# A long-convolution and SwiGLU kernel: orders and issue times from a table, first-norm statistics on DVE, weights in column pieces

## The chip, the cores and the metric

One core of one Trainium2 chip. Times are device microseconds (us) of one execution. "PE" is TensorE (matmul), "PEld" its weight loads, "DVE" VectorE, "ACT" ScalarE, "POOL" GpSimd, "SP" SyncE, which here only issues DMAs. A time is the median of several executions; a ratio is the mean time of one kernel's fast runs over the mean of the other's fast runs in the same rounds, so it is not quite the ratio of the medians quoted beside it. The calls in which kernels were run together were made on different chips, so kernels of different calls are compared by their ratios to the kernel before. One rule of reading: a PE that is "busy" in the profile is not a PE at its peak, so I also count *PE work*, the matmul columns of a stretch divided by 2,400 per us. The rate is the 2.4 GHz that the Trainium skill states ("TensorE: Matmul & The Clock Gate", Part 1). The trace agrees: in the stretches that PE fills, it does 9.7 to 10.05 us of such work per 10 us. The whole kernel has 251.5 us of it.

## The reference

```python
def _A_ref(q, k, v, shift_k, ssm_k, ssm_D):       # S = 2048, D = 640, bf16
    k_shift = sum over t of k_pad[:, t:t+S] * shift_k[:, 3 - t]      # 4 taps
    kv = k_shift * v
    y = irfft(rfft(pad(kv)) * rfft(pad(ssm_k)))[:S]                  # causal long convolution
    return q * (y + kv * ssm_D)

x  = A_q
h  = x + _A_ref(layernorm(x), A_k, A_v, A_shift_k, A_ssm_k, A_ssm_D)
n  = layernorm(h)
h2 = h + (silu(n @ w_gate) * (n @ w_up)) @ w_down                    # F = 1728
```

## The kernel before: what the change touches

The sequence is worked in four blocks j of 512 positions, each in two column halves c of 320. A block's convolution is a chain: load k and v, form `kv` on DVE, a first transform on PE, evict it, re-shuffle it between partitions by DMA (`sb<-sb`), a second transform, evict, swap the partition halves by DMA, complex products on DVE, two inverse transforms with another re-shuffle between. Then come the residual, the second norm, transposes, and the FFN, whose gate and up matmuls are 512 columns wide. A block's FFN can't begin before its convolution ends, and the FFN is 175 of the 251.5 us of PE work. In the first stage of the kernel there is no FFN work, and PE can only wait for the chain.

The program is a list of operations with priorities and dependences. A scheduler inside the kernel's builder simulates the engines and fixes each engine's order; the engines then run in that order and wait for each other by semaphores.

```python
def schedule(self, dma_model, bias):          # greedy list scheduling at build time
    ...
    for e in ("pe", "dve", "act", "sp", "pool"):
        if free[e] > t + 1e-9: continue
        best = None
        for o in ready:                        # the ready operation of least priority number
            ...
        o.eng, o.start = e, t
        ...

def ln_act(l, j, prio):                        # first norm: statistics on ACT, two passes
    for b in range(4):
        ... a.activation(out=junk, in_=x_b, func=ACTF.Copy, accum_out=sum_b)
    ...                                        # negative mean on DVE
    for b in range(4):
        ... a.activation(out=junk, in_=x_b, func=ACTF.Square, bias=negm_b, accum_out=ss_b)
    ln_rstd(l, j, prio, True, range(4))

def load_weights():                            # on the Pool queue, at most two on their way
    for i in range(5):                         # pieces of 128 rows: each gate group needs all five
        for (nm, t, wd) in (("wg", WG, B_w_gate), ("wu", WU, B_w_up)):
            piece([(V(t, i * FM, FM), dram(wd, i * 128 * F, [[F, 128], [1, FM]]))], 426, [(t, i)], ...)
    ...                                        # last 64 columns, then w_down

def group(t, bank, w, st, col, ...):           # one gate or up group: 5 matmuls of 512 columns
    wr = ... [(w, d) for d in range(5)]        # waits for all five row pieces
```

## Time and profile before

The kernel before takes 342.67 us (342.43 to 344.55, three runs).

| | before |
|---|---|
| PE busy | 286.1 us, 83% |
| DVE busy | 236.5 us, 69% |
| ACT busy | 202.3 us, 59% |
| first matmul of 512 columns (FFN) | 96.1 us |
| PE work done by 96 us | 28.2 of 251.5 us |

The page of the kernel before, part 2: 40 slices of 8.6 us. A digit is the busy share in tenths, in PEclk the granted clock in tenths.

```profile
PE   2161675867688999899799999999989999999992
DVE  0876453579883999889899899988888481222320
ACT  4175974886979877594278967766396521222100
PEclk9996656695589999999999999999999999999997
DMA  7949999898534556526546432634701101000011
```

Through the first eleven slices PE is partly idle, and from the fourth to the eleventh its clock is mostly granted only in part, while the DMA engines are nearly full up to the tenth. From the 14th slice on PE is nearly full.

The same in three stretches, from the table of windows (after the stretch: length, then busy us and number of instructions of PE, PEld, DVE, ACT, POOL, then granted clock, DMA share, GB/s):

```profile
0.00:96.00 96.00, 53.91 (x252) 24.93 (x253) 60.19 (x94) 65.07 (x108) 30.39 (x44) 0.74 0.82 255
96.00:118.00 22.00, 19.98 (x103) 9.41 (x102) 15.56 (x25) 19.11 (x33) 1.96 (x2) 0.98 0.44 135
118.00:284.00 166.00, 159.76 (x1012) 92.36 (x1011) 147.01 (x236) 109.58 (x170) 16.90 (x20) 1.00 0.43 127
```

PE is "busy" for 53.9 us of the first 96 and does 28.2 us of work in them. The low clock accounts for part of that: 53.9 us at a granted share of 0.74 are 40 us at full clock. The rest is the rule of reading above. What it waits for between 20 and 100 us, from the waits (total us, times, longest):

```profile
PE ps L537 <- DMA sb<-sb: 16.5, 9, 6.4
PE ps L537 <- ACT sb L522: 8.4, 17, 1.2
```

The shuffles are the longest wait. Pairing issues and landings in the trace, a shuffle issued between 20 and 60 us lands after a median 4.8 us, and after 2.4 us from 200 us on. The groups of the two norms' statistics (count, busy us, mean ns, idle before):

```profile
L788 ACT ACTIVATE sb<-sb,stt 128x640 bf16<-128x640 bf16 x16 | 13.1, 824 | 2.4 <-DVE stt L784 2.4
L781 ACT ACTIVATE sb<-sb 128x640 bf16<-128x640 bf16 x16 | 11.6, 727 | 2.1 <-DMA sb<-in_A_q_dram 2.0
L743 DVE BATCH_NORM_STATS2 stt<-sb 128x6 f32<-128x320 bf16 x32 | 14.0, 478 | 0.1
```

### The profile page before, as it was taken

What the parts mean: (1) busy time and instruction counts of PE and PEld (TensorE: products, weight loads), DVE (VectorE), ACT (ScalarE), POOL (GpSimd) and SP (SyncE); (2) the same over time, 40 slices, a digit from 0 to 9 for tenths busy, and PEclk for the clock granted to TensorE, in tenths of its full rate; (3) what the DMA queues carried; (4) which work ended last, traced back from release to release, by engine and by line L of the source; (5) the groups of instructions that cost most, each with busy time, mean ns of one, the idle gap of its engine ahead of it and who ended that gap; (6) DMA issues with size and microseconds to landing.
All of it is one profiled execution on the core that took longest, in us unless ns stands there. A gap on an engine that the chain in (4) does not pass through costs nothing. (4 is left out here: it accounts for less than half of the span.)

```text
span 343.3 us, 4790 instructions
## 1 busy us (share of the span) xinstructions
PE 286.1 (83%) x1668; PEld 156.3 (46%) x1668; DVE 236.5 (69%) x367; ACT 202.3 (59%) x317; POOL 49.2 (14%) x66
## 2 busy tenths in 40 slices
PE   2161675867688999899799999999989999999992
PEld 0140222332343565467554445576444477444571
DVE  0876453579883999889899899988888481222320
ACT  4175974886979877594278967766396521222100
POOL 4332513331211022021000100020001010000000
PEclk9996656695589999999999999999999999999997
DMA  7949999898534556526546432634701101000011
GB/s 194 397 138 327 298 254 305 257 287 246 143 124 142 126 183 213 150 77 193 162 156 191 123 125 74 197 134 136 184 28 38 38 21 38 21 0 0 3 38 39
DMA packets 27196, 49.78 MB, mean 145 GB/s; under 512 B 3858, under 2 KB 19123, under 8 KB 27045
## 3 DMA queue, kind: packets, MB, share of 16 engines
q1 hardware_dynamic: 22130, 32.29, 30.1%
q0 software_dynamic: 4064, 16.37, 16.4%
q10 hardware_dynamic: 978, 0.82, 1.0%
q8 instruction: 13, 0.21, 0.3%
q14 instruction: 11, 0.09, 0.1%
HBM read 20.63 MB, written 2.62 MB: 68 GB/s over the span
## 5 line engine op out<-in xcount | busy, mean ns | idle before, releaser
L537 PE MATMUL ps<-sb 128*128 128x512 bf16 (+2 forms) x996 | 192.1, 344 | 4.0 <-DMA sb<-in_A_shift_k_dram 2.5
L546 DVE TENSOR_TENSOR sb<-sb 128x1280 bf16<-128x1280 bf16 (+1 forms) x208 | 158.8, 798 | 29.1 <-DMA sb<-in_A_k_dram 11.3
L522 ACT ACTIVATE sb<-ps 128x640 bf16<-128x640 f32 (+1 forms) x144 | 101.8, 750 | 54.3 <-PE ps L537 37.4
L537 PEld LDWEIGHTS ps<-sb 128*128 128x128 bf16 (+1 forms) x996 | 97.0, 98 | 79.5 <-DMA sb<-in_A_shift_k_dram 2.4
L537 PE MATMUL ps<-sb,tab 128*128 128x320 bf16 x496 | 101.2, 340 | 32.8 <-DMA sb<-sb 18.6
L546 DVE TENSOR_TENSOR sb<-ps,sb 128x640 bf16<-128x640 f32 (+2 forms) x64 | 60.3, 950 | 54.7 <-PE ps L537 48.2
L537 PEld LDWEIGHTS ps<-sb,tab 128*128 128x128 f16 x496 | 47.4, 106 | 82.4 <-DMA sb<-sb 23.6
L982 ACT ACTIVATE sb<-ps 128x1024 bf16<-128x1024 f32 (+2 forms) x32 | 29.2, 912 | 40.8 <-PE ps L537 40.8
L769 ACT ACTIVATE sb<-sb,stt 128x320 bf16<-128x320 bf16 (+1 forms) x43 | 29.3, 728 | 10.0 <-DVE stt L761 8.1
L759 POOL TENSOR_TENSOR stt<-stt 128x2 f32<-128x2 f32 (+1 forms) x12 | 13.0, 1082 | 106.1 <-DVE stt L758 106.0
L525 ACT ACTIVATE sb<-ps 128x640 bf16<-128x640 f32 x32 | 21.6, 700 | 4.5 <-PE ps L537 4.5
L640 PE MATMUL ps<-sb 128*128 128x128 bf16 x96 | 7.9, 242 | 11.6 <-DMA sb<-in_A_ssm_k_dram 11.6
L788 ACT ACTIVATE sb<-sb,stt 128x640 bf16<-128x640 bf16 x16 | 13.1, 824 | 2.4 <-DVE stt L784 2.4
L743 DVE BATCH_NORM_STATS2 stt<-sb 128x6 f32<-128x320 bf16 x32 | 14.0, 478 | 0.1
L640 PEld LDWEIGHTS ps<-sb 128*128 128x128 bf16 x96 | 6.9, 121 | 13.3 <-DMA sb<-in_A_ssm_k_dram 12.5
L781 ACT ACTIVATE sb<-sb 128x640 bf16<-128x640 bf16 x16 | 11.6, 727 | 2.1 <-DMA sb<-in_A_q_dram 2.0
L530 POOL DMA_DIRECT2D sb<-in_A_ssm_k_dram x12 | 7.8, 654 | 33.4 <-PE ps L640 26.6
L942 PE MATMUL ps<-sb 128*128 128x128 bf16 x80 | 6.9, 243 | 2.4 <-ACT sb L522 1.9
L530 POOL DMA_DIRECT2D sb<-in_A_k_dram x6 | 5.9, 982 | 18.9 <-DVE sb L546 18.9
L530 POOL DMA_DIRECT2D sb<-in_A_v_dram x6 | 4.7, 791 | 22.4 <-PE ps L537 22.4
L942 PEld LDWEIGHTS ps<-sb 128*128 128x128 bf16 x80 | 5.5, 109 | 5.0 <-ACT sb L522 3.9
L761 DVE TENSOR_TENSOR stt<-stt 128x2 f32<-128x2 f32 (+1 forms) x12 | 1.9, 156 | 5.9 <-POOL stt L759 5.8
(25 smaller groups left out, 38.9 us busy)
## 6 DMA issues: line engine op xcount, KB each, us to landing
sb<-sb SPq DMA_DIRECT2D x160, 160.0 KB, 3.1
sb<-in_A_k_dram POOLq DMA_DIRECT2D x6, 560.0 KB, 6.7
out_dram<-sb SPq DMA_DIRECT2D x16, 160.0 KB, 1.8
sb<-in_B_w_gate_dram POOLq DMA_DIRECT2D x5, 416.0 KB, 4.4
sb<-in_B_w_up_dram POOLq DMA_DIRECT2D x5, 416.0 KB, 5.6
sb<-in_A_v_dram POOLq DMA_DIRECT2D x6, 320.0 KB, 4.0
sb<-in_A_q_dram POOLq DMA_DIRECT2D x3, 640.0 KB, 7.2
sb<-in_A_ssm_k_dram POOLq DMA_DIRECT2D x6, 256.0 KB, 4.2
```

The source lines that it names most:

```text
L522: fns = {"act": lambda a: a.activation(out=dst(), in_=src(), func=ACTF.Copy), "dve": lambda v: v.tensor_copy(out=dst(), in_=src())}
L525: fns = {"act": lambda a: a.activation(out=dst(), in_=src(), func=ACTF.Copy, scale=scale), "dve": lambda v: v.tensor_scalar(out=dst(), in0 ...
L530: fns = [(lambda g, d=d, s=s: g.dma_start(d(), s())) for d, s in subs]
L537: return lambda t: t.matmul(o(), l(), r(), start=st, stop=sp)
L546: return lambda v: v.tensor_tensor(out=o(), in0=a(), in1=b_(), op=op)
L640: return t.transpose(B16(pt, b // 2, (b % 2) * CW + o_, 128), src, V(IDN, 0, 128))
L743: vec(dve1(CW, False), lambda v: v.bn_stats(st6(l, j, b, c), V(xt, b * D + c * CW, CW)), [(xt, (b, c))], [(ST, ("s", l, j % 2, b, c))], pr ...
L759: P.op({"pool": 0.4}, lambda g: g.tensor_tensor(out=y, in0=va, in1=stt[:, 288:288 + hi - lo], op=ALU.pow), c1 + [(ST, "half")], c3, prio, ...
L769: "act": lambda a: a.activation(out=dst(), in_=src(), func=ACTF.Identity, scale=rs(l, j, b), bias=tmv(l, j, 3)[:, b:b + 1])},
L788: P.op({"act": act_c(D) + 0.3}, lambda a, b=b, jt=jt: a.activation(out=V(jt, 0, D), in_=V(xt, b * D, D), func=ACTF.Square, bias=tmv(l, j, ...
L942: fns.append(lambda t, k=k, d=d: t.transpose(B16(pt, k, d * 128, 128), V(hn[k], d * 128, 128), V(IDN, 0, 128)))
L982: P.op({"act": act_c(n)}, lambda a: a.activation(out=dst(), in_=src(), func=ACTF.Silu), rd, wr, -1000, name=f"si{j}{i}")
```

## The change

Its intent: replace the greedy scheduler by orders found beforehand. Engine and planned start of each of the 1,227 operations come from a table in the source. The first norm's statistics move from ACT to DVE (`bn_stats`, as the second norm has them). The gate and up weights come in four column pieces each, so that a group waits only for its own columns, and most loads move from the Pool queue into SP's queue, among the shuffles. The old rule that at most two weight pieces are on their way goes too.

```diff
-    def schedule(self, dma_model, bias):
-        ...                                             # 90 lines of simulation
+    def replay(self, table):
+        raw = np.frombuffer(zlib.decompress(base64.b85decode(table)), np.uint8)
+        eng, start = raw[:n], raw[n:].view(np.uint16)
+        for o, e, s in zip(self.ops, eng, start):
+            o.eng, o.start = self.ENG[e], 0.01 * int(s)
+        ...                                             # orders and buffer slots by planned start
+        for o in self.ops:                              # pacing of transfers
+            if o.dma is None or o.start < 1.5: continue
+            held = [...]                                # planned ends of what it waits for anyway,
+            ...                                         # and of the entry before it in its queue
+            if held and max(held) > o.start - 1.0: continue
+            ...
+                o.deps.setdefault(self.ops[work[k][1]], 2)
-        def ln_act(l, j, prio):                         # Copy and Square with accumulation on ACT
+        def ln_x(j, prio):                              # bn_stats and aggregation on DVE
+            for b in range(4):
+                for c in range(2):
+                    ln_stats(0, j, b, c, xts[j], prio)
+            ln_dve(0, j, prio, range(4))
-            for i in range(5):                          # five row pieces each
+            for f0, f1 in ((0, 3), (3, 6), (6, 9), (9, 13)):      # four column pieces each
+                n = (f1 - f0) * 128
                 for (nm, t, wd) in (("wg", WG, B_w_gate), ("wu", WU, B_w_up)):
+                    piece([(V2(t, f0 * 128, FM, 5, n), dram(wd, f0 * 128, [[F, 128], [128 * F, 5], [1, n]]))], ...)
-                wr = ... else [(w, d) for d in range(5)]
+                wr = ... else [(w, col // 128)]
```

## The prediction

> **What bounds the kernel now (342.67 us).** Matmul columns counted by shape from the trace (540 of 512, 944 of 320, the rest 128), divided by the 2.4 GHz that the Trainium skill states ("TensorE: Matmul & The Clock Gate", Part 1), give an estimate of 251 us of TensorE work at full clock. The table of windows shows three stages:
>
> - 0 to 96 us, before the first FFN matmul: only 30 us of that work is done. From 20 to 96 us the granted clock is 0.67, PE 48 of 76 us busy, DVE 49, ACT 59, the DMA engines 82%. In the waits, PE stands longest for sb<-sb shuffles (16.5 us), which take a median 4.8 us to land from 20 to 60 us, 2.4 to 2.8 after 100: they share the DMA engines with 6.6 MB of weights. Critical is the chain of block 0 (shuffles, ACT evictions of 0.70 us, two norms).
> - 96 to 284 us: clock 1.00, DVE 163 of 188 us busy, TensorE doing 9 to 10 us of work per 10: PE and DVE limit together.
> - 284 us to the end: the last FFN, PE alone, then 6.5 us of final add, store and closing.
>
> **What the change does.**
>
> - First-norm statistics leave ACT: 16 Copy (0.73), 16 Square (0.82), 32 accumulator reads (0.19), about 31 us. DVE gains 32 bn_stats (0.48, 0.40 back to back) and 16 aggregations (0.17), about 15 us. The table gives DVE 423 operations; 367 plus these 48 is 415, so some 8 evictions or norms move there, about 5 us. DVE goes from 236.5 to about 257, ACT from 202 to about 165.
> - Weights come in column pieces, 768 to 1,024 bytes a run instead of 3,328; a gate group waits for its own columns only. Loads wait on planned compute, most on SP. The skill, "DMA: Bandwidth & Descriptors" (Issuing engines are not separate DMA queues), says that all share the same 16 engines, so I expect gain from timing, not bandwidth.
> - Ordering the PE operations by the table's planned starts, the first FFN group comes after 27 us of PE work instead of 30, block 0's transposes after 24 instead of 28; FFN groups alternate with convolution from there. Before the last block's transposes lie 207 us, after them 45 (now 53).
>
> **Where it lies on the path.** The gain is in the first stage: block 0 finishes at 68 to 75 us rather than 90, because ACT and the DMA engines are freed, and PE becomes full that much earlier. With the first FFN matmul at 72, 180 us of PE work at 95% lead to the last transposes at 262 to 268; 45 plus 7 give 314 to 320. DVE contradicts mildly: from 9.2 us, 242 us of work before the last transposes and 20 to 25 us of idle (now 52) give 272 to 276, thus 324 to 328. DVE takes over as the limit and eats part of the gain.
>
> **Prediction: 321 us, range 308 to 334. Faster by over 2%: 0.88; within: 0.09; slower: 0.03.**
>
> **What would show it.** First 512-column matmul near 72 us, clock 1.0 from there; no Square or accumulator reads on ACT; DVE about 257 us, over 80%; early shuffles landing in 3.5 us; weights landing until beyond 90 us; no PE wait for weights; a final FFN-only stretch of 45 us.
>
> **What would make it wrong.** DVE packed better than I allow (under 310); DMA landing later than planned, shuffles behind paced loads on SP's in-order queue (above 335); short descriptors making the weights late.

## The result

The changed kernel takes 327.69 us (324.61 to 328.75, four runs), ratio to the kernel before 0.9538 (0.9465 to 0.9611). It was run again, as `after_again` (325.26 us, ratio 0.9467) and `after_third` (327.66 us, 0.9542). Its own spread, 324 to 330 us, is wider than the effect of some experiments below.

| | before | after |
|---|---|---|
| PE busy | 286.1 us, 83% | 279.8 us, 86% |
| DVE busy | 236.5 us, 69% | 251.3 us, 77% |
| ACT busy | 202.3 us, 59% | 172.8 us, 53% |
| first FFN matmul | 96.1 us | 78.0 us |
| PE work done by 96 us | 28.2 us | 43.8 us |
| span of the profiled run | 343.3 us | 326.9 us |

The page after, part 2 (slices of 8.2 us):

```profile
PE   2366588549997499999999999998999999999992
DVE  1499989996981979999999989989998976024421
ACT  3068589874987158547477567774355302321100
PEclk9999769957999699999999999999999999999997
DMA  7957979896989346537562621555531200100001
```

PE reaches its first nine in the tenth slice (the 14th before), and DVE is nearly full from the third slice on. But in the 13th and 14th slices PE falls to 7 and 4, with a dip of the clock, and DVE to 1 in the 13th. The windows, same stretches as before:

```profile
0.00:96.00 96.00, 64.42 (x348) 32.50 (x349) 77.92 (x138) 65.42 (x97) 15.24 (x22) 0.88 0.84 258
96.00:118.00 22.00, 14.91 (x81) 7.88 (x80) 12.62 (x19) 10.77 (x17) 1.11 (x2) 0.84 0.62 157
118.00:284.00 166.00, 163.30 (x1033) 95.38 (x1031) 148.72 (x256) 92.05 (x128) 12.16 (x11) 1.00 0.41 126
```

By 96 us the changed kernel is 15.7 us of PE work ahead (43.8 less 28.2); its profiled span is 16.4 us shorter. So nearly the whole gain is made in the first stage, as predicted. It would be more, but for 96 to 118 us: PE is 14.9 us busy there, against 20.0 before. This profile is of the slowest of the four runs; the same stretch in the profile of `after_third`, the fastest of its six, is milder:

```profile
96.00:118.00 22.00, 17.58 (x99) 9.38 (x98) 16.04 (x24) 13.84 (x20) 2.25 (x4) 0.92 0.66 194
```

PE's waits between 20 and 100 us have shrunk:

```profile
PE ps L454 <- DMA sb<-sb: 6.8, 6, 1.9
PE ps L454 <- ACT sb L438: 6.8, 15, 0.9
```

Shuffles issued between 20 and 60 us now land after a median 2.6 us (4.8 before). The smaller pieces alone do not do it: with them under the greedy scheduler (`parts_greedy` below) the median is 6.0 us, and with row pieces under the table (`rows_table`) 3.5. The statistics are all on DVE, 64 instead of 32:

```profile
L660 DVE BATCH_NORM_STATS2 stt<-sb 128x6 f32<-128x320 bf16 x64 | 29.7, 482 | 0.1
```

**The stall.** The chain of waits, followed back from the last instruction, goes through it (start, us, what):

```profile
93.21 2.75 SPq L446
95.96 0.04 issue
96.00 9.53 DMA sb<-sb
105.53 0.02 issue
105.55 0.83 DVE sb L463
```

A swap is issued in two halves. SP needs 2.75 us to issue the first (its median is 0.58), so that the second is issued at 96.00 only, and this lands 9.5 us later. The timeline says what DVE and PE do meanwhile (start, us, engine, line, what, in brackets the idle time before and who ended it):

```profile
100.50 0.83 DVE L463 TENSOR_TENSOR sb<-sb 128x1280 bf16<-128x1280 bf16 x1 [2.95 <-DMA sb<-sb]
105.55 0.83 DVE L463 TENSOR_TENSOR sb<-sb 128x1280 bf16<-128x1280 bf16 x1 [4.22 <-DMA sb<-sb]
...
110.89 2.31 PE L454 MATMUL ps<-sb,tab 128*128 128x320 bf16 x8 [7.09 <-DVE sb L463]
```

And the loads issued around this swap:

```profile
89.82 0.59 SPq L446 DMA_DIRECT2D sb<-in_B_w_down_dram  x1
90.51 0.56 SPq L446 DMA_DIRECT2D sb<-sb  x1
91.17 0.54 SPq L446 DMA_DIRECT2D sb<-in_A_k_dram  x1
91.81 4.82 SPq L446 DMA_DIRECT2D sb<-sb  x4
93.29 1.29 POOL L446 DMA_DIRECT2D sb<-in_A_ssm_k_dram  x2 [8.28 <-PE ps L557]
94.58 0.87 POOL L446 DMA_DIRECT2D sb<-in_B_w_up_dram  x1
95.45 0.78 POOL L446 DMA_DIRECT2D sb<-in_B_w_down_dram  x1
96.23 0.89 POOL L446 DMA_DIRECT2D sb<-in_B_w_gate_dram  x1
96.67 0.59 SPq L446 DMA_DIRECT2D sb<-in_B_w_up_dram  x1
```

From the k load at 91.17 us on these are 2.1 MB of loads, with the swaps' own halves 2.8 MB, issued within 6 us, and a table of narrower windows has the DMA share at 1.01 from 92 to 107 us. From 107 to 118 it is 0.16.

**Plan against chip.** Each operation's planned start is in the table, so I could pair plan and trace operation by operation. This is the slip (measured start less planned start, us) of some PE operations in three runs; the last column, `best2`, is the best of the experiments.

```
operation                        planned   after   after_third    best2           
first filter transpose, block 0      5.3     5.8       5.6            5.9
a second transform, block 0, c=1    31.3     8.2       8.2            5.0
first transposes, block 0           60.5     9.9       9.5            6.6
first gate group, block 0           66.0    12.0      11.9           10.0
inverse of block 1, c=1             91.4    20.6      17.7           11.3
first transposes, block 1          128.9    23.0      19.7           14.0
first transposes, block 3          247.5    25.6      22.7           16.8
```

The plan is not a prediction of mine, it is part of the kernel; but the slip shows where the chip falls behind it. That is almost only before 118 us, while loads are on their way: 5.8 us by the first transpose, 6 more by the first gate group, 6 to 9 more from there to block 1's inverse, which is the stall. In the 120 us between the first transposes of block 1 and of block 3 only 3 are added.

**The pacing code does nothing.** The change's text says that loads are paced, and the code adds a wait on a compute operation to a transfer that has over 1 us of planned slack. I built the program and counted: of 192 transfers none gets such a wait, because for each the entry before it in its queue, or something it has to wait for anyway, is planned to end within 1 us of its start (three start too early to be asked). What paces the loads is their place in the queues among the shuffles.

### The profile page after: what moved, and what is told of

Its sections match the earlier page's. It is cut to its first block, busy times and chain, and to the rows that moved or that the text cites. A ratio compares the mean times of both kernels' runs of the same rounds, so it can differ in the third digit from the quotient of the medians.

```text
span 326.9 us, 4728 instructions
## 1 busy us (share of the span) xinstructions
PE 279.8 (86%) x1668; PEld 156.4 (48%) x1668; DVE 251.3 (77%) x423; ACT 172.8 (53%) x245; POOL 28.5 (9%) x34
## 3 DMA queue, kind: packets, MB, share of 16 engines
q1 hardware_dynamic: 37682, 45.17, 45.5%
## 4 chain that ended last, share of the span: by engine, by line
PE 55%; DVE 12%; DMA 11%; ACT 10%; issue 5%; SPq 4%; POOL 2%; ACTq 0%; DVEq 0%
PE ps L454 53%; DVE sb L463 10%; DMA sb<-sb 9%; ACT sb L438 8%; SPq L446 3%; DMA sb<-in_A_ssm_k_dram 3%; POOL stt L676 2%; DVE stt L660 1%; PE ps L848 1%; PE ps L557 1%; ACT sb L686 1%; ACT sb L892 1%; ACT sb L441 0%; ACT L892 0%; DVE stt L664 0%
## 5 line engine op out<-in xcount | busy, mean ns | idle before, releaser
L438 ACT ACTIVATE sb<-ps 128x640 bf16<-128x640 f32 (+1 forms) x140 | 97.7, 745 | 59.1 <-PE ps L454 55.4
L454 PE MATMUL ps<-sb,tab 128*128 128x320 bf16 x496 | 95.4, 326 | 28.0 <-DVE sb L463 10.1
L463 DVE TENSOR_TENSOR sb<-ps,sb 128x640 bf16<-128x640 f32 (+3 forms) x64 | 60.7, 952 | 36.8 <-PE ps L454 35.4
L686 ACT ACTIVATE sb<-sb,stt 128x320 bf16<-128x320 bf16 (+1 forms) x40 | 28.4, 734 | 16.8 <-DVE stt L678 15.0
L660 DVE BATCH_NORM_STATS2 stt<-sb 128x6 f32<-128x320 bf16 x64 | 29.7, 482 | 0.1
L676 POOL TENSOR_TENSOR stt<-stt 128x2 f32<-128x2 f32 (+1 forms) x12 | 14.6, 1223 | 149.7 <-DVE stt L675 106.9
L439 DVE COPY sb<-ps 128x1280 bf16<-128x1280 bf16 x6 | 4.9, 822 | 11.7 <-PE ps L557 7.9
L446 POOL DMA_DIRECT2D sb<-in_A_ssm_k_dram x6 | 4.1, 680 | 47.2 <-PE ps L557 30.0
L664 DVE BATCH_NORM_AGGREGATE stt<-stt 128x2 f32<-128x12 f32 x32 | 5.5, 192 | 0.0
L439 DVE CAST sb<-ps 128x640 bf16<-128x640 f32 x2 | 1.6, 824 | 3.5 <-PE ps L454 3.4
L564 POOL TENSOR_TENSOR sb<-sb 1x320 bf16<-1x320 bf16 x2 | 2.0, 1012 | 17.5 <-DVE sb L439 10.9
```

What stands on the lines that cost most here:

```text
L438: fns = {"act": lambda a: a.activation(out=dst(), in_=src(), func=ACTF.Copy), "dve": lambda v: v.tensor_copy(out=dst(), in_=src())}
L439: "dve": lambda v: v.tensor_copy(out=dst(), in_=src())}
L446: fns = [(lambda g, d=d, s=s: g.dma_start(d(), s())) for d, s in subs]
L454: return lambda t: t.matmul(o(), l(), r(), start=st, stop=sp)
L463: return lambda v: v.tensor_tensor(out=o(), in0=a(), in1=b_(), op=op)
L660: vec(dve1(CW, False), lambda v: v.bn_stats(st6(l, j, b, c), V(xt, b * D + c * CW, CW)), [(xt, (b, c))], [(ST, ("s", j % 2, b, c))], prio, ...
```

## The experiments

Two theories stood after the traces. Theory A: the gain comes from orders and issue times, and what is missing from it is lost where loads collide with shuffles and swaps on the DMA engines. Theory B, the prediction's own: DVE has become the limit, and DMA waits only show where it has slack. A third, for the gain, was the freed ACT.

Twelve runs follow. All were reported correct within the tolerance, also the one whose statistics are wrong. `MOVE` is a small dictionary of planned starts that overrides the table: `o.start = self.MOVE.get(o.name, 0.01 * int(s))`. All else stays as the table has it, so it changes an order, and for a load with over 1 us of slack it also makes the pacing wait come into being. In its names, `ident` is the identity matrix, `x` the input, `kin` a load of k, `kraw` of the raw filter, `wg`, `wu` and `wd` gate, up and down pieces, `gul0` and `gul1` the last 64 columns of up and gate, and `kte00` the first eviction of the filter's transposes.

### One part alone: first-norm statistics on DVE, greedy scheduler kept

```diff
 (kernel before)
-            ln_act(0, j, pb + (300 if j else 95))
+            ln_x(j, pb + (300 if j else 95))
```

> The kernel before with its own greedy list scheduling, and only the first norm's statistics taken to DVE (32 bn_stats and 16 aggregations in place of 16 Copy, 16 Square and their accumulator reads on ACT). Theory A (most of the gain is in the orders and in when loads are issued): between 1% faster and 1% slower, 339 to 346 us. Rival (freeing 31 us of ACT in the first stage is the gain): 8 us or more faster, under 335.

342.54 us, ratio 0.9958 (0.9877 to 1.0039; one slow run of four left out of the ratio). Its page shows the trade in the busy times:

```profile
PE 280.7 (83%) x1650; PEld 155.5 (46%) x1668; DVE 246.6 (73%) x415; ACT 179.5 (53%) x253; POOL 46.2 (14%) x66
```

23 us less on ACT and 10 more on DVE give nothing. Under the old scheduler the rival, that ACT was the gain, falls. The table with the statistics left on ACT was not tried.

### Two parts: column pieces as well, greedy scheduler kept

```diff
 (the version above)
-            for i in range(5):   ... five row pieces
+            for f0, f1 in ((0, 3), (3, 6), (6, 9), (9, 13)):   ... four column pieces
-                wr = ... [(w, d) for d in range(5)]
+                wr = ... [(w, col // 128)]
```

> The same plus the column pieces of the weights, still greedy. Theory A: all weights had landed at 75 us in the kernel before, well ahead of the first FFN matmul at 96, so pieces alone give nothing: within 2 us of the norm-only version. Rival (a gate group that waits only for its columns starts the FFN earlier): 4 us or more faster than the norm-only version.

341.54 us, ratio 0.9960 (0.9902 to 1.0019): within 1 us of the version above. Under the old scheduler the pieces are worth nothing, since all the weights had landed at 75 us, well before the first FFN matmul at 96. So the rest of the change makes the step from 0.996 to 0.954: the table with its orders, its issue times (with the end of the limit of two weight pieces) and SP's queue for the loads, alone or together with the two parts. These were not separated from each other.

### Column pieces undone under the table

```diff
 (kernel after)
-            for f0, f1 in ((0, 3), (3, 6), (6, 9), (9, 13)):   ... columns
+            for d0, d1 in ((0, 1), (1, 2), (2, 3), (3, 5)):    ... rows
-                wr = ... [(w, col // 128)]
+                wr = ... [(w, d) for d in range(5)]
+    MOVE = {'wg2': 47.0, 'wu2': 56.0}
```

> The changed kernel with row pieces of the weights again (runs of 3,328 bytes, every gate group waits for all eight); two pieces had to be planned earlier (at 47 and 56 us) since the order deadlocks otherwise. Theory A (the pieces matter only because they let the loads spread past the first FFN matmul): 0.85 MB more are loaded before the first FFN group, it starts 2 to 5 us later than in the changed kernel, total 1 to 6 us more. Rival (longer runs move faster and outweigh it): the same or less than the changed kernel.

329.50 us, ratio 0.9595, against 0.9538, 0.9467 and 0.9542 of the changed kernel: 0.5 to 1.3% slower, 2 to 4 us. It was run at another time. The intervals overlap, so the size is not certain; but the trace has the first gate group 5 us later (slip 17.1 us, against 12.0 and 11.9), as expected. Without the two moves the check for deadlocks refused the program: the table plans pieces of the weights after the first gate groups, and with row pieces these wait for them. The column pieces are thus what allows the table its late loads, and, as it seems, are worth a little only there.

### The start: the identity first

The first filter transpose is planned at 5.3 us and runs at 11.06. I took the identity matrix, which lands at 10.97 us behind the filter on ACT's queue, for the cause.

```diff
+    MOVE = {"ident": 0.6, "x0": 5.6, "kin10": 6.2}
```

> The identity matrix is issued first on ACT's queue, and the x and second k loads after the first v and filter loads. Theory A (the plan has the first transposes at 5.3 us, they start at 11.06 because identity and filter land at 10.97 and 9.92; all that follows inherits about 5 us): the first transposes at 8 to 10 us, everything 1 to 3 us earlier, total 1 to 3 us less than the changed kernel. Theory B (first-stage shifts are absorbed by slack before the FFN): within 1 us.

A miss. 325.06 us, ratio 0.9487, within the changed kernel's own spread (0.9467). The identity landed at 2.6 us, but the second part of the filter load now landed at 11.17 us instead of 9.92, and the transposes began at 11.2 us as ever. So which of the two was issued first does not matter. The DMA engines are full meanwhile (a share of 1.02 from 2 to 11 us, here and in the changed kernel), so the bytes that share them are the likely limit; no run took any away.

### The stall: six loads behind the swaps

```diff
+    MOVE = {"kin30": 81.0, "wu6": 83.0, "kraw21": 86.0, "wd6": 99.0, "gul1": 100.5, "gul0": 101.5}
```

> Six loads (k of block 3, raw filter of block 2, three weight pieces, one of them the small last up and gate columns) are planned after the two swaps at 92 to 97 us instead of around them. Theory A (the swap lands 12 us after its issue because 2.8 MB of loads share the DMA engines with it, and PE and DVE then stand for it): the swap lands within 5 us, the PE gap at 100 to 118 us shrinks by 7 to 10 us, total 317 to 321 us. Theory B (DVE's own work limits from here, the DMA wait only shows where slack is): total within 2 us of the changed kernel, 325 to 329, with DVE filling the gap.

323.46 us, ratio 0.9424, against 0.9467 of the changed kernel: 1.5 us less in the mean of the fast runs, which the intervals don't separate. The mechanism came out as theory A said: the swap was issued at 92.5 and landed at 97.1 us, and the slip of PE at block 1's inverse fell from 20.6 (17.7 in another run of the changed kernel) to 12.8 us. The size did not, because I had moved two small loads too far. A new wait shows in PE's waits:

```profile
PE ps L455 <- DMA sb<-in_B_w_up_dram: 3.2, 1, 3.2
```

That is the last gate group waiting for the last 64 columns of the weights. The down piece and these two had run into the next shuffles, and PE lost another 1.7 us right after.

### Only the two smallest of these loads later

```diff
+    MOVE = {"gul0": 101.5, "gul1": 100.5}
```

> Only the two smallest of those loads (82 KB each, runs of 128 bytes) are planned later. Theory A (bytes in the burst decide): little, 0 to 2 us off the changed kernel. Rival C (the many tiny runs of 128 bytes clog the queues): most of the gain of the six-load version, 5 us or more.

326.26 us, ratio 0.9525: no gain. The swap still needed 9.1 us to land, from 91.8 to 100.9. That the tiny runs of these two make the stall is ruled out as far as the swap's landing tells.

### DVE: more work, and less

```diff
 (kernel after, more)
+            if l == 0:                       # a second bn_stats into an unused place
+                fns.insert(0, lambda v: v.bn_stats(unused, V(xt, b * D + c * CW, CW)))
 (kernel after, less; wrong result on purpose)
-  v.bn_stats(st6(l, j, b, c), V(xt, b * D + c * CW, CW))
+  v.bn_stats(st6(l, j, b, c), V(xt, b * D + c * CW, CW if l else 16))
```

> The changed kernel with every one of the first norm's 32 bn_stats done twice (the extra result goes to an unused place): about 13 us more of DVE work. The prediction's theory (DVE takes over as the limit, only 20 to 25 us of it idle before the last transposes): total 10 to 13 us more. Theory A (after 118 us PE is the limit and the time lost is DMA waits): under 6 us more.

334.39 us, ratio 0.9748, which is 2.1 to 2.8 points above the changed kernel's ratios, 7 to 10 us. It was run at another time. DVE was busy 262.9 us, 11.6 more. So neither number was right: too much for theory A, too little for a pure DVE limit. (The edit also makes each of these operations wait for the last but one; DVE's idle time did not grow by it, as the numbers below show.)

> Wrong result on purpose: the first norm's 32 bn_stats read 16 elements instead of 320, which takes some 9 us of work from DVE. 11.6 us of added DVE work cost 7 to 10 us. If DVE is a full co-limit (theory B), as much is won back per us: 5 to 8 us less than the changed kernel. If DVE had only small slack and PE or DMA limits just below (theory A): 0 to 3 us less.

325.59 us, ratio 0.9484, against 0.9542 of the changed kernel: 2.0 us less in the mean, which the intervals don't separate, for 9.3 us less of DVE (242.1 busy). Here theory A's number held. Added DVE work costs 0.6 to 0.8 us per us, removed work returns 0.2. The traces tell where. From 9.2 us to block 0's first FFN transposes, DVE is busy 54.5 of 61.2 us in the changed kernel. With the added work it is busy 61.2 of 65.9, and these transposes come at 75.1 us instead of 70.4 (69.9 in `after_third`): most of the delay is made there. With work removed it is busy 50.0 of 61.1, and they come at 70.3, no earlier. So DVE has some 2 us of slack in the chain of block 0: more work uses it up and delays the chain, while less work only leaves DVE to wait for something else. In this run the swap of the stall was still issued at 92.8 and landed at 102.6 us.

### The changed kernel once more, for comparison

> The changed kernel unaltered, for comparison on the same chip. Both theories: 324 to 329 us, and again a stall of PE between about 96 and 118 us in which the last swap (sb<-sb) of block 1's second column half lands over 8 us after its issue.

325.26 us, ratio 0.9467. One of its four executions, the profiled one, took 1,574.82 us, left out of the ratio, though not of the median (the three fast runs have a mean of 324.86 us); see the last section. So this run's own profile can't tell of the stall.

> The changed kernel unaltered once more, as the base of this call: 324 to 329 us.

327.66 us, ratio 0.9542. In its profiled run, of 324.0 us, the swap landed 9.6 us after its issue (12.3 in the first profile of the changed kernel, of 326.9 us). The stall is there in each profile of a fast run, and its length varies: in `after_third` SP issued both halves in 0.59 us each, and PE's longest wait was 4.4 us, so some 2 of the 2.7 us between the two correspond to the slow issue of 2.75 us.

### Two sets of moves

```diff
+    MOVE = {"gul0": 13.0, "gul1": 13.3, "wg9": 45.6, "kin30": 81.0, "wu6": 83.0,
+            "kraw21": 86.0, "wd6": 104.0, "kte00": 9.2}
```

> Moves of planned starts only. The two small last-column loads go to 13 us, where the DMA engines were 61% busy; the last gate piece (655 KB) from 28 to 45.6 planned; the k load of block 3, the filter of block 2 and one up piece behind the swaps; one down piece far behind; and the first filter eviction on DVE behind the first two products, which were ready earlier. The six-load version removed the 96 to 118 us stall but made the last gate group wait 3.2 us for the small pieces and pushed bytes into the next swaps. Theory A (collisions of loads with swaps and shuffles): 4 to 8 us under the changed kernel of this call. Theory B (DVE's work limits): 0 to 2 us under it.

324.42 us, ratio 0.9459, against 0.9542: 2.9 us less in the mean of the fast runs (the intervals overlap), under what theory A had asked for. The swap landed after 3.9 us and the first stall was gone, but two others had opened. The gate piece moved to 45.6 delayed the shuffles at 55 us (the slip there rose from 6.5 to 10.0 us at once), and at 118 to 128 us two down pieces, block 3's k and two swaps met:

```profile
118.00:130.00 12.00, 8.13 (x37) 3.82 (x35) 7.74 (x11) 4.84 (x8) 0.00 (x0) 0.86 0.90 234
```

PE is busy 8.1 us of 12 there, with the DMA engines at 0.90. Loads moved out of one collision had run into the next.

```diff
+    MOVE = {"gul0": 13.0, "gul1": 13.3, "kin30": 81.0, "wu6": 83.0, "wg9": 85.0, "kraw21": 87.5,
+            "wd6": 97.8, "kin31": 112.0, "wd3": 92.0, "kte00": 9.2}
```

> The first set of moves took the stall at 96 to 118 us away, but a second one of some 5 us opened at 118 to 128 us, where two down pieces, block 3's k and two swaps met, and the 655 KB gate piece, moved to 45.6, cost as much near 55 us as it won near 35. This set puts that gate piece at 85, one down piece at 92, one at 97.8, and block 3's second k load at 112 planned. Theory A (collisions, each avoidable while the DMA engines have quiet stretches): both stalls gone, ratio to the kernel before 0.930 to 0.942, about 319 to 323 us. Rival (the DMA engines are so full before 118 us that every move opens another stall): 0.944 to 0.954, no better than the first set, with a new wait of PE or DVE of 4 us or more on a shuffle elsewhere.

318.41 us (316.68 to 319.94), ratio 0.9292 (0.9256 to 0.9328), the interval clear of all others. This version beats both kernels: 24 us less than the kernel before, and by the ratios 6 to 9 less than the changed one. It was run at another time. No operation was changed, only the places of nine loads and one eviction; six of the moved loads now have enough planned slack to get the pacing wait. Its windows:

```profile
0.00:96.00 96.00, 64.06 (x357) 33.38 (x358) 79.01 (x141) 67.10 (x99) 14.31 (x20) 0.88 0.85 261
96.00:118.00 22.00, 19.69 (x117) 10.47 (x116) 18.72 (x26) 15.45 (x24) 3.32 (x5) 1.00 0.93 264
118.00:284.00 166.00, 163.91 (x1024) 95.23 (x1023) 143.00 (x248) 87.85 (x121) 10.86 (x9) 1.00 0.37 110
```

From 96 to 118 us the DMA engines are *busier* than in the changed kernel (0.93 against 0.62, or 0.66 in `after_third`), and PE is busy 19.7 us instead of 14.9 (17.6), at full clock. The loads now fill the quiet time that the stall had left behind it. The swap was issued at 90.9 and landed at 94.6 us. The rival, that the DMA engines are too full for any move to help, falls. Not every term is separated: the eviction moved on DVE and the two small loads at 13 us came in both sets, and the slip at 36 us fell from 8.2 to 5.0 us there. What each of the ten moves is worth alone was not tried, nor the moves without the pacing waits that they brought into being.

## Why the prediction was right, and what in it was not

The time, 327.7 us, lay within the range of 308 to 334, and the gain was 15 us instead of 21.7.

- **"The gain is in the first stage" — right.** 15.7 us more PE work is done by 96 us, of a gain of 16.4 in the profiled runs.
- **"Because ACT and the DMA engines are freed" — half wrong.** Freeing ACT under the greedy scheduler gave 0.4%, within the noise. The DMA engines are not freed: 82% of the first 96 us before, 84% after. What changed under the table is that the early shuffles land in 2.6 instead of 4.8 us, and that more work is done early: DVE does 77.9 instead of 60.2 us in these 96 (9.5 of the 17.7 more are statistics and their aggregations).
- **"First 512-column matmul near 72 us" — 6 us too early.** It came at 78.0. The plan has the first gate group at 66.0 and the slip had grown to 12 us there: 5.8 at the first transposes, which wait for the first loads, the rest after them. That this rest is shuffles and swaps behind loads was not tested one by one.
- **The term that was left out: the stall at 96 to 118 us.** The prediction held "shuffles behind paced loads" only as a risk that would end above 335. It happened, at a smaller size: PE was busy 14.9 of 22 us. From the first FFN matmul to the last block's transposes PE needed 195 us for 177.5 us of work, 91% where I had put 180 us at 95%. Of the 17.5 us lost, 9.8 lie between 96 and 118 us (6.2 in `after_third`); from 118 to 284 us it did 159.2 us of work in 166, 96%.
- **"DVE takes over as the limit and eats part of the gain" — half right.** Added DVE work cost 0.6 to 0.8 us per us, so there is little slack. But it was not what held the changed kernel at 327: with the same DVE work the last set of moves runs at 318, and with 9.3 us less of it the kernel gained only 2.0. That the DVE path's 324 to 328 us hit the measured 327.7 is partly luck: it had 242 us of work from 9.2 us to the last block's transposes and 20 to 25 idle, and the trace has 235.5 and 28.4, so that two errors cancel (273.1 us, where it had 272 to 276). In the last set of moves 20.5 us of idle remain, and the transposes come at 264.3.
- **"Loads wait on planned compute" — wrong.** No transfer of the changed kernel gets such a wait; the order in the queue paces them.
- **"So I expect gain from timing, not bandwidth" — right.** The packets of the queues that carry the program's transfers took 47.5% of 16 engines' 343.3 us before and 50.2% of 326.9 after, 163 and 164 us: the shorter runs cost about nothing. "DMA: Bandwidth & Descriptors" (Issuing engines are not separate DMA queues) says that all queues end on the same 16 engines, and the stall fits it: the swap on SP's queue landed in 4.6 us instead of 12.3 once loads on both queues had been moved behind it (no run moved those of the Pool queue alone).
- Sizes that held: DVE 251.3 us busy (257 predicted; 77% where I said over 80), ACT 172.8 (165), the final stretch of FFN alone 45.5 us (45), no wait of PE for weights. The "30 us" of work that the prediction gives the first 96 us of the kernel before are 28.2 by the columns.

Open: how much of the table's gain is order, how much issue time and how much the change of queue; what holds the chain of block 0 when DVE has less to do; why one issue on SP took 2.75 us in one profile and 0.59 in another; and whether the statistics' move is worth more under the table than the nothing it was worth under the old scheduler.

## What to carry to other kernels

When a chain of DMA shuffles sets the pace, ask of every bulk load which shuffle it will meet: 2.1 MB of loads issued within 6 us around two swaps left PE idle for 7.1 us in one profile and 4.4 in another, and moving nine loads and one eviction was worth 6 to 9 us, while the statistics' move and the column pieces gave nothing clear of noise under the old scheduler. If a planned schedule exists, pair it with the trace operation by operation; the places where the slip grows are the list of things to mend, and a moved load must be followed to the next collision. And check in the built program that a mechanism which a change announces, here the pacing waits, is there at all.

## What the Trainium skill lacked or had wrong

- "DMA: Bandwidth & Descriptors" gives the time of a transfer by its size and names arbitration between queues, but no time for a small transfer that meets bulk loads. Here a 160 KB shuffle lands in 2.0 us at best, in a median 4.8 us beside the weights in the kernel before, and a swap 12.3 us after the start of its issue in the stall.
- The same page's back-pressure text is about remote DMA. Here the *issue* of a local DMA can be held up too: SP took 2.75 us for one issue in the stall (median 0.58). Why is open: the same issue took 0.59 us in `after_third`, and single issues of 1.2 to 1.6 us came at 155 to 160 us too, where the DMA engines were busy to about 0.3.
- The same page (Specifications) asks for runs of 512 bytes or more for line rate. Above it the trace of the changed kernel still shows a loss: a packet of 640 bytes took a median 32 ns, of 1,280 bytes 55, of 4,096 bytes 159, which is 20, 23 and 26 bytes per ns of one engine. The packets of 2,560 bytes don't fit this row: a median of 169 ns, 15 bytes per ns.
- No page has the duration of the norm statistics on DVE: 0.48 us for 128 x 320 bf16, 0.17 to 0.19 us for the aggregation. None has that of an accumulator read on ACT: 0.19 us each, beside an activation of 0.73 us.
- "TensorE: Matmul & The Clock Gate" warns (Part 1, "HAM trace caveats"; HAM is the monitor that gates the clock) that the clock records can be unreliable and the clock stuck at a quarter for over 50 us. One execution may be such a case, far longer, though no record of its clock shows it: it was of the changed kernel and took 1,574.82 us, with PE busy 99%, a mean matmul of 1,479 ns instead of 345 (128x512 and 128x320 together) and a weight load of 321 ns instead of 98, DVE's times unchanged, and a recorded granted clock of 1.0. It came once and its cause is open; no run here tells.
